# The seven products of a Strassen-Winograd unit summed in PSUM on ScalarE's copies, with two sums left to VectorE

## The chip, the cores and the metric

One core of one Trainium2 chip runs the whole program in one launch. The metric is device time in microseconds (us), from the core's own clock; three runs of the kernel before gave 543.16, 543.61 and 543.85 us, median 543.61. A profile is one execution, and its span runs from the first instruction to the last.

## The reference, cut to what matters

```python
# attention, batch 2, 12 heads, 448 tokens, head dimension 64, causal
attn = softmax(where(mask, -1e9, q @ k.T / 8)); x = (attn @ v)   # -> 896 x 768
# gated layer: 768 -> 1536 -> 768
xn = x / sqrt(mean(x * x) + 1e-6) * rms_g
x = (silu(xn @ w_gate) * (xn @ w_val)) @ w_out
# bilinear layer: 768 -> 1024, then two linear maps
h = ((x @ w1) * (x @ w2)) @ w3
return h @ w_out                                              # 896 x 768, float32
```

## The kernel before, in words

Tokens lie along the free axis: a tile is 128 features by 448 tokens of one batch, and everything after attention comes in such tiles. Every float32 operand is split into a high float16 part and a low bfloat16 part, and a product of two operands is three matmuls (high·high, high·low, low·high). `halve` makes the parts of a tile (`hi_part`, L448, on ScalarE or VectorE; `lo_part`, L452/L453, on VectorE or GpSimd).

The two layers' first maps and the very last one come as 2x2 blocks: two blocks of weights (gate and value, or w1 and w2) by two batches. `wino` (L832) computes such a 2x2 block product by the Strassen-Winograd scheme in 7 products in place of 8. There are 23 of these units: 12 of the gated layer (`unit`, weights `wgv`; called the gate stage), 8 of the bilinear layer (`wab`; the bilinear stage) and 3 at the end (`funit`; the last stage). A product of the first 20 units is 9 matmuls of 128x448 columns, of the last three 12. `w_out` of the gated layer between them (the `wo` stage) is computed plainly, in 12 groups of 36 matmuls. A unit's weights are loaded as 64-bit words, rebuilt to float32 (`fetch`, L464 to L473: a DMA, two VectorE operations and one that runs on ScalarE at L469 or on VectorE at L471), summed into the weights' Winograd combinations (`sums`, through `tt`: L487 on VectorE, L488 on GpSimd) and halved.

`wino` before: each of the seven products goes into its own PSUM bank (`mm_b`, eight banks in turn). ScalarE copies the first product to SBUF (`evict`, L847), and VectorE adds the others to running sums in SBUF (`join`, L850): seven joins in a unit, five of the products joined once and one of them twice. So a product waits for its bank to be free and for nothing else of its unit.

W' = w3 @ w_out does not depend on the input rows and is computed beside attention (`w_prime`; 16 groups of 24 matmuls of 128x384, all in the one bank of `g_b`, evicted by ScalarE at L521). The attention of a pair of heads (`pair`) is twelve calls; `norm(b)` closes a batch: it takes the row norms (squares at L673 on ScalarE), transposes the rows on TensorE, and forms the batch's inputs `xs` and their combinations (L705, L710, L736). `mix` does the same after the `wo` stage.

What sets the order: nothing is issued in the order of the source. `add` records each operation with an engine (some with a second one), an estimated duration, what it reads and writes, and a priority. `Plan.order` is a list scheduler: it runs a forward pass and a backward pass alternately (`PASSES` = 8 times), keeps the best, and issues every operation in the planned order. TP, WP0, WPS, GVS, OS, AS, FS and the dictionary PO hold the starting priorities; they were fitted together. Every engine then works through its own queue in that fixed order.

Of the kernel before, what the change touches and what calls it, by code (L numbers as in the profile page):

```python
# [40 lines left out]
TP = 27.6196  # L41
WP0 = -239.098
WPS = 45.6507
GVS = 3.3215
OS = 5.5733
AS = 2.8104
FS = -2.3605
PO = dict(dq=75.1441, dv=-34.3235, vh=-105.6002, vl=46.2211, sc=-50.0374, s3=-49.1818, hA=-126.5569,
    hl=33.2591, hB=-20.1561, pv=4.1734, sq=-72.0513, nm=15.7476, wm=1.3462, ww=-44.1947, wx=4.9061,
    g=68.9761, a=-39.7332, o=0.6949, f=-24.4064, gm=-31.525, e=-8.003, ae=-133.6189, y=-21.9007,  # L50
    t1=-54.0072, mx=44.5005, dw=-92.7682)
# [213 lines left out]
def actp_us(n):  # L265
    return n * 0.00083 + 0.055
# [14 lines left out]
def fused_kernel(ctx: ExitStack, tc, qk, v, g, wgv, wo, wab, w3t, wout, out):  # L281
# [208 lines left out]
    def mm(*a, **k):  # L490
        nc.tensor.matmul(*a, **k)  # L491
# [278 lines left out]
    def mm_group(ps, kp, terms, n, prio):  # L770
        for c in range(0, len(terms), n):
            def f(c=c):
                for q in range(c, min(c + n, len(terms))):
                    a, bb = terms[q][0]
                    k = 3 * q
                    for x0, x1 in ((a[0], bb[0]), (a[0], bb[1]), (a[1], bb[0])):
                        mm(ps[:, :S], x0, x1, start=(k == 0), stop=(k == 3 * len(terms) - 1))
                        k += 1
            ch = terms[c:c + n]
            add("pe", 3 * len(ch) * mm_us(S), f, r=[k for t in ch for k in t[1]], w=[kp], prio=prio)  # L780

# [49 lines left out]

    def wino(w, x, n, pr):  # L832

        (e1, k1), (c11, k11) = kp_r.next(), kp_r.next()
        (u3, k3), (c22, k22), (c21, k21) = (ew_r.next() for _ in range(3))

        def prod(ws, s, p):
            ps, kp = mm_b.next()
# [4 lines left out]
            mm_group(ps, kp, terms, 3, p)  # L843
            return ps[:, :S], kp

        def evict(dst, kd, ps, kp, p):
            add("act", actp_us(S), lambda: nc.scalar.activation(dst, ps, AF.Copy), r=[kp], w=[kd], prio=p)  # L847

        def join(dst, kd, ps, kp, y, ky, p):
            add("dve", dve_us(S), lambda: nc.vector.tensor_tensor(dst, ps, y, op=ALU.add), r=[kp, ky], w=[kd], prio=p)  # L850

        evict(e1, k1, *prod(0, 0, pr), pr)
        join(c11, k11, *prod(1, 1, pr), e1, k1, pr)
        pr += PO["gm"]
        join(e1, k1, *prod(4, 4, pr), e1, k1, pr)
        join(u3, k3, *prod(5, 5, pr), e1, k1, pr)
        five = prod(3, 3, pr)
        join(c22, k22, *five, u3, k3, pr)
        join(e1, k1, *five, e1, k1, pr)
# [126 lines left out]
```

## Time and profile before

| | before |
|---|---|
| median of three runs (lowest, highest) | 543.61 us (543.16, 543.85) |
| span of the profiled execution | 540.7 us |
| what the median has beside that span | 2.9 us |
| instructions | 9343 |
| TensorE (PE) busy | 527.1 us, 97%, 3516 matmuls |
| VectorE (DVE) busy | 487.1 us, 90%, 923 |
| ScalarE (ACT) busy | 363.6 us, 67%, 540 |
| GpSimd (POOL) busy | 179.3 us, 33%, 137 |
| mean granted TensorE clock | 1.000 |

The profiled execution's own time is told by its span alone; the 2.9 us are the launch and the end around it, by the runs' median.

How to read it: a busy share is a mean over stages. PE at 97% means little by itself, since matmuls are pipelined and their ends are modelled; whether PE really works at its pace is seen from the number of matmuls in a stretch, and whether it waits is seen from the list of waits and the chain. On the chain, a piece "PE x1926" means that PE went from one matmul to the next 1926 times without waiting for anyone.

### The profile page before, as it was taken

To read this page: it belongs to the slowest core of one execution; us is meant where nothing else is said; L and a number is where in the kernel's file an instruction comes from. 1 tells how busy PE (TensorE), PEld (TensorE's weight loads), DVE (VectorE), ACT (ScalarE), POOL (GpSimd) and SP (SyncE) were. 2 spreads that over 40 slices of the span, in tenths; PEclk is the share of its full clock that TensorE was granted. 3 is DMA by queue.
4 is the path that set the end of the run, shared out by engine and by line. 5 is a ranking of instruction groups with operands and counts; after the bars stand their busy time and mean duration, and the time that the engine had idled before them with its cause. 6 is when DMAs were issued, how large, how long until landed. Compare 5 with 4: busy or idle time off the path is not lost.

```text
span 540.7 us, 9343 instructions
## 1 busy us (share of the span) xinstructions
PE 527.1 (97%) x3516; PEld 293.4 (54%) x3516; DVE 487.1 (90%) x923; ACT 363.6 (67%) x540; POOL 179.3 (33%) x137
## 2 busy tenths in 40 slices
PE   8899999999988999999999999999999999999997
PEld 6556566565655555555555555555555555555553
DVE  6889999999958999999999998889769999999943
ACT  6899999999768766758565778797336543453310
POOL 4001214144226727573853310000100734556300
PEclk9999999999999999999999999999999999999999
DMA  8886768999931152433333347525105111000121
GB/s 277 303 300 210 258 246 184 239 234 202 204 99 58 59 176 73 161 116 117 118 118 116 118 176 241 226 91 203 58 1 174 60 60 58 1 0 1 52 86 68
DMA packets 46813, 74.92 MB, mean 139 GB/s; under 512 B 31408, under 2 KB 32944, under 8 KB 46768
## 3 DMA queue, kind: packets, MB, share of 16 engines
q1 hardware_dynamic: 46768, 74.33, 45.1%
q8 instruction: 27, 0.44, 0.3%
q14 instruction: 18, 0.15, 0.1%
HBM read 64.23 MB, written 2.75 MB: 124 GB/s over the span
## 4 chain that ended last, share of the span: by engine, by line
PE 81%; DVE 7%; ACT 5%; DMA 4%; issue 2%; SPq 0%; ACTq 0%; DVEq 0%
PE bank L491 80%; DMA st<-in_wout 2%; DVE arena L452 1%; ACT st L469 1%; PE bank L600 1%; ACT arena L448 1%; DMA arena<-arena 1%; DVE arena L560 1%; DVE cv L473 1%; DMA st<-in_wgv 1%; DVE cv L466 1%; DMA arena<-in_v 1%; ACT arena L736 1%; ACT arena L564 1%; ACT arena L673 0%
## 5 line engine op out<-in xcount | busy, mean ns | idle before, releaser
L491 PE MATMUL bank<-arena 128*128 128x448 f16 (+10 forms) x2976 | 441.8, 315 | 7.0 <-DVE arena L560 2.5
L491 PEld LDWEIGHTS <-arena 128*128 128x128 f16 x3048 | 249.7, 98 | 218.6 <-issue 15.1
L469 ACT ACTIVATE st<-st 128x768 uint16<-128x768 uint16 (+2 forms) x75 | 120.8, 1645 | 25.8 <-DVE cv L466 23.2
L850 DVE TENSOR_TENSOR arena<-bank,arena 128x448 f32<-128x448 f32 x161 | 91.3, 611 | 15.1 <-PE bank L491 14.7
L448 ACT ACTIVATE arena<-arena 128x448 f16<-128x448 f32 (+2 forms) x96 | 57.0, 612 | 35.9 <-DVE arena L487 27.2
L473 DVE SCALAR_TENSOR_TENSOR cv<-st,cv 128x768 int32<-128x768 int32 (+2 forms) x84 | 72.7, 868 | 5.1 <-ACT st L469 4.4
L453 POOL TENSOR_TENSOR arena<-cv,arena 128x384 bf16<-128x384 f32 (+2 forms) x29 | 46.1, 1590 | 86.8 <-ACT arena L448 77.8
L491 PE MATMUL bank<-xs,arena 128*128 128x448 f16 x360 | 72.5, 352 | 2.0 <-DVE arena L705 2.0
L448 ACT ACTIVATE arena<-cv 128x384 f16<-128x384 f32 (+2 forms) x82 | 54.0, 670 | 23.7 <-PE bank L491 11.9
L453 POOL TENSOR_TENSOR arena<-arena 128x448 bf16<-128x448 f32 (+2 forms) x32 | 46.6, 1468 | 49.4 <-ACT arena L448 40.7
L466 DVE TENSOR_SCALAR cv<-st 128x768 int32<-128x768 int32 (+2 forms) x84 | 45.3, 547 | 12.2 <-DMA st<-in_wout 4.4
L452 DVE TENSOR_TENSOR arena<-arena 128x448 bf16<-128x448 f32 (+2 forms) x68 | 50.5, 753 | 1.8 <-ACT arena L448 1.4
L448 ACT ACTIVATE arena<-st 128x1536 f16<-128x1536 f32 (+1 forms) x25 | 34.4, 1381 | 19.5 <-DVE st L487 9.9
L452 DVE TENSOR_TENSOR arena<-cv,arena 128x384 bf16<-128x384 f32 (+2 forms) x55 | 44.2, 815 | 0.2 <-ACT arena L448 0.2
L564 ACT ACTIVATE arena<-arena 128x128 f32<-128x128 f32 (+3 forms) x84 | 41.6, 520 | 2.8 <-DVE arena L560 2.2
L487 DVE TENSOR_TENSOR arena<-arena 128x448 f32<-128x448 f32 x53 | 35.2, 677 | 3.8 <-ACT arena L896 3.8
L488 POOL TENSOR_TENSOR st<-cv,st 128x384 f32<-128x384 f32 x8 | 10.8, 1353 | 78.3 <-DVE st L487 78.3
L560 DVE CUSTOM_DVE_ANT_0 arena<-bank,arena 128x128 f32<-128x128 f32 (+3 forms) x84 | 35.9, 443 | 0.4 <-ACT arena L564 0.3
L452 DVE TENSOR_TENSOR arena<-st,arena 128x1536 bf16<-128x1536 f32 (+1 forms) x21 | 35.3, 1679 | 0.1
L491 PEld LDWEIGHTS bank<-arena 64*128 64x128 f32 (+2 forms) x288 | 25.8, 178 | 16.5 <-DVE arena L560 5.0
L488 POOL TENSOR_TENSOR arena<-arena 128x448 f32<-128x448 f32 x18 | 24.9, 1388 | 14.6 <-ACT arena L871 5.8
L871 ACT ACTIVATE arena<-arena 128x448 f32<-128x448 f32 x24 | 13.7, 575 | 19.1 <-DVE arena L850 19.0
(67 smaller groups left out, 311.3 us busy)
## 6 DMA issues: line engine op xcount, KB each, us to landing
st<-in_wgv SPq DMA_DIRECT2D x24, 768.0 KB, 4.4
st<-in_wab SPq DMA_DIRECT2D x16, 768.0 KB, 4.4
st<-in_wo SPq DMA_DIRECT2D x12, 768.0 KB, 5.8
st<-in_w3t SPq DMA_DIRECT2D x16, 512.0 KB, 5.1
st<-in_wout SPq DMA_DIRECT2D x16, 384.0 KB, 3.8
arena<-in_qk SPq DMA_DIRECT2D x12, 448.0 KB, 5.4
arena<-in_v SPq DMA_DIRECT2D x12, 256.0 KB, 3.7
out_t<-arena SPq DMA_DIRECT2D x12, 224.0 KB, 1.9
```

The lines of the kernel that those rows point to most:

```text
L448: add("act", act_us(n), lambda: nc.scalar.activation(hi, src, AF.Copy), r=r, w=w, prio=prio, alt=(("dve", dve2_us(n), lambda: nc.vector.te ...
L452: add("dve", dve_us(n), lambda: nc.vector.tensor_tensor(lo, src, hi, op=ALU.subtract), r=r, w=w, prio=prio, port=True, alt=(("pool", pool_ ...
L453: port=True, alt=(("pool", pool_us(n), lambda: nc.gpsimd.tensor_tensor(lo, src, hi, op=ALU.subtract)),))
L466: add("dve", dve2_us(n), lambda: nc.vector.tensor_scalar(cv, hi, 3, 0x3FFFFFFF, op0=ALU.logical_shift_left, op1=ALU.bitwise_and), r=[ks], ...
L469: add("act", ACT_TOP * n - 0.08, lambda: nc.scalar.activation(b[:, :, 2], b[:, :, 1], AF.Copy, scale=1.0 / 8192, bias=-8191.0 / 16384), w= ...
L473: add("dve", dve_us(n), lambda: nc.vector.scalar_tensor_tensor(cv, hi, -0x3FFFFFF9, cv, op0=ALU.bitwise_and, op1=ALU.bitwise_or), r=[ks], ...
L487: add("dve", dve_us(n), lambda: nc.vector.tensor_tensor(out, a, b, op=op), port=True, alt=(("pool", pool_us(n) + 0.1, lambda: nc.gpsimd.te ...
L488: ("pool", pool_us(n) + 0.1, lambda: nc.gpsimd.tensor_tensor(out, a, b, op=op)),), **kw)
L491: nc.tensor.matmul(*a, **k)
L560: add("dve", dve_us(w), lambda: nc.vector.tensor_tensor_reduce(out=sc[:, :w], in0=ss[:, :w], in1=m, scale=-CSC, scalar=3.0e38, op0=ALU.add ...
L564: add("act", act_us(w) + 0.1, lambda: nc.scalar.activation(dst, sc[:, :w], AF.Exp, bias=mx[:, c:c + 1], scale=-1.0), r=[ksc, kmx + (c,)], ...
L850: add("dve", dve_us(S), lambda: nc.vector.tensor_tensor(dst, ps, y, op=ALU.add), r=[kp, ky], w=[kd], prio=p)
```

## The change

`wino` takes five banks A, E, B, C, D for a unit. Product 0 starts A. ScalarE copies A into bank B (a `fork`, PSUM to PSUM). Product 3 goes to E, and ScalarE copies it out to SBUF as m3. Product 4 is accumulated on A (`fresh=False`: its first matmul doesn't clear the bank), a second fork copies A into C, product 1 is accumulated on B, product 5 on A, a third fork copies A into D, product 6 is accumulated on C, product 2 on D. B and D are then two finished blocks that lie in PSUM; VectorE adds m3 to C and to A, which gives the other two. The products' arithmetic order changes, not their number.

A matmul that accumulates needs the bank's written marks to be set. Where no matmul of these stages has written the target bank yet, one matmul is put ahead of the fork (`primed`); this happens for four banks in the whole program.

What follows a unit changes with it. In the gate stage the Silu of batch 0 reads PSUM and writes SBUF, and the multiplication of batch 0 (`times`) reads PSUM, so that it runs on VectorE alone; batch 1 is as before. In the bilinear stage ScalarE first copies batch 0's block to SBUF; in the last stage it copies two blocks to SBUF ahead of their DMA. All starting priorities have new values, and two are added (`fk` for forks, `pm` for the marking matmuls).

```diff
-TP = 27.6196
-WP0 = -239.098
-WPS = 45.6507
-GVS = 3.3215
...
+TP = 25.3479
+WP0 = -234.519
+WPS = 43.9438
+GVS = 8.3892
...
-    def mm_group(ps, kp, terms, n, prio):
+    primed = set()
+
+    def mm_group(ps, kp, terms, n, prio, fresh=True):
...
-                        mm(ps[:, :S], x0, x1, start=(k == 0), stop=(k == 3 * len(terms) - 1))
+                        mm(ps[:, :S], x0, x1, start=(fresh and k == 0), stop=(k == 3 * len(terms) - 1),
+                           skip_group_check=True)
                         k += 1
...
+        primed.add(kp)
...
+    def copy_out(dst, kd, ps, kp, p, func=AF.Copy, r=()):
+        add("act", actp_us(S), lambda: nc.scalar.activation(dst, ps[:, :S], func), r=[kp, *r], w=[kd], prio=p)
+
     def wino(w, x, n, pr):
 
-        (e1, k1), (c11, k11) = kp_r.next(), kp_r.next()
-        (u3, k3), (c22, k22), (c21, k21) = (ew_r.next() for _ in range(3))
-
-        def prod(ws, s, p):
-            ps, kp = mm_b.next()
+        A, E, B, C, D = (mm_b.next() for _ in range(5))
+        m3, k3 = ew_r.next()
+
+        def prod(ws, s, dst, fresh, p):
...
-            mm_group(ps, kp, terms, 3, p)
-            return ps[:, :S], kp
...
-        evict(e1, k1, *prod(0, 0, pr), pr)
-        join(c11, k11, *prod(1, 1, pr), e1, k1, pr)
+            mm_group(*dst, terms, 3, p, fresh)
+
+        def fork(dst, src, p):
+            if dst[1] not in primed:
+
+                primed.add(dst[1])
+                (wi, kw), (x0, kx0) = w(0, 0), x(0, 0, 0)
+                add("pe", mm_us(S), lambda: mm(dst[0][:, :S], wi[0], x0, start=True, stop=True,
+                                                skip_group_check=True),
+                    r=[*kw, kx0], w=[dst[1]], prio=p + PO["pm"])
+            add("act", actp_us(S), lambda: nc.scalar.activation(dst[0][:, :S], src[0][:, :S], AF.Copy),
+                r=[src[1]], w=[dst[1]], prio=p + PO["fk"])
...
+        prod(0, 0, A, True, pr)
+        fork(B, A, pr)
+        prod(3, 3, E, True, pr)
+        copy_out(m3, k3, *E, pr)
         pr += PO["gm"]
-        join(e1, k1, *prod(4, 4, pr), e1, k1, pr)
-        join(u3, k3, *prod(5, 5, pr), e1, k1, pr)
-        five = prod(3, 3, pr)
-        join(c22, k22, *five, u3, k3, pr)
-        join(e1, k1, *five, e1, k1, pr)
-        join(c21, k21, *prod(2, 6, pr), u3, k3, pr)
-        join(e1, k1, *prod(6, 2, pr), e1, k1, pr)
-        return (c11, k11), (c21, k21), (e1, k1), (c22, k22)
+        prod(4, 4, A, False, pr)
+        fork(C, A, pr)
+        prod(1, 1, B, False, pr)
+        prod(5, 5, A, False, pr)
+        fork(D, A, pr)
+        prod(6, 2, C, False, pr)
+        prod(2, 6, D, False, pr)
+        return B, D, join(*C, pr, kp_r), join(*A, pr, ew_r)
+
+    def times(e, ke, u, ku, pr):
+        add("dve", dve_us(S), lambda: nc.vector.tensor_tensor(e, u[:, :S], e, op=ALU.mult), r=[ku], w=[ke], prio=pr)
...
+        e, ke = kp_r.next()
+        copy_out(e, ke, g0, kg0, pr, AF.Silu, ["exp"])
+        add("act", act_us(S), lambda g1=g1: nc.scalar.activation(g1, g1, AF.Silu), r=["exp"], w=[kg1], prio=pr)
+        times(e, ke, u0, ku0, pr)
+        tt(g1, u1, g1, ALU.mult, r=[ku1], w=[kg1], prio=pr)
```

## Rows read from the trace of the kernel before

**Rows 1.** The page's first part: engine, busy us (share of the span), instructions.
```profile
PE 527.1 (97%) x3516; PEld 293.4 (54%) x3516; DVE 487.1 (90%) x923; ACT 363.6 (67%) x540; POOL 179.3 (33%) x137
```
**Rows 2.** The chain that ended last, in order of time: start, us, what.
```profile
30.19 9.46 PE bank L491 x70
...
157.03 0.38 ACT wpr L521
157.42 0.04 issue
157.46 4.07 PE bank L491 x24
...
172.65 364.51 PE bank L491 x1926
537.18 0.62 DVE arena L850
```
**Rows 3.** Everything that PE waited for: us in total, times, longest.
```profile
PE bank L491 <- DVE arena L560: 2.5, 3, 1.7
PE bank L491 <- DVE arena L705: 2.0, 1, 2.0
PE bank L491 <- ACT wpr L521: 1.9, 3, 0.9
PE bank L491 <- DMA arena<-arena: 1.5, 2, 1.1
```
**Rows 4.** Stages: start:end, length, then each engine's busy us (and instructions).
```profile
0.00:30.19 30.19, 25.77 (x183) 17.45 (x184) 22.84 (x57) 23.92 (x38) 5.56 (x19) 1.00 0.88 297
30.19:81.42 51.23, 51.23 (x448) 31.48 (x448) 48.91 (x146) 49.79 (x88) 8.82 (x8) 1.00 0.74 246
81.42:172.65 91.23, 85.59 (x962) 56.14 (x961) 80.95 (x219) 78.65 (x163) 35.46 (x29) 1.00 0.81 180
172.65:312.00 139.35, 139.35 (x737) 72.11 (x737) 137.71 (x199) 93.35 (x114) 78.61 (x50) 1.00 0.34 114
312.00:394.00 82.00, 82.00 (x436) 42.39 (x434) 70.07 (x106) 59.47 (x67) 3.66 (x2) 1.00 0.46 164
394.00:490.00 96.00, 96.00 (x509) 49.68 (x508) 92.44 (x144) 46.81 (x59) 37.79 (x24) 1.00 0.15 50
490.00:537.20 47.20, 47.14 (x250) 24.17 (x247) 33.60 (x57) 11.66 (x16) 9.41 (x8) 1.00 0.15 55
```
**Rows 5.** Groups by shape, whole span: line, engine, shapes, count, busy us, mean ns.
```profile
L850 DVE TENSOR_TENSOR arena<-bank,arena 128x448 f32<-128x448 f32 x161 | 91.3, 611 | 15.1 <-PE bank L491 14.7
L847 ACT ACTIVATE arena<-bank 128x448 f32<-128x448 f32 x23 | 12.9, 559 | 19.0 <-PE bank L491 18.1 <-DVE arena L452 0.5 <-POOL arena L453 0.4
L521 ACT ACTIVATE wpr<-bank 128x384 f32<-128x384 f32 x16 | 7.9, 494 | 0.4 <-PE bank L491 0.4
L736 ACT ACTIVATE arena<-bank,gcol 128x448 f32<-128x448 f32 x9 | 5.7, 636 | 0.2 <-DVE xs L705 0.2
```
**Rows 6.** ScalarE's longest groups in the gate stage alone, 172.65 to 312.
```profile
L469 ACT ACTIVATE st<-st 128x768 uint16<-128x768 uint16 x18 | 34.4, 1940 | 11.3 <-DVE cv L466 10.9
L448 ACT ACTIVATE arena<-st 128x1536 f16<-128x1536 f32 x10 | 14.8, 1491 | 7.2 <-DVE st L487 7.1
```
**Rows 7.** Timeline at one copy of a first product: start, us, engine, what.
```profile
435.78 0.92 PE L491 MATMUL bank<-xs,arena 128*128 128x448 f16 x4
...
436.53 1.87 PE L491 MATMUL bank<-arena 128*128 128x448 f16 x9
436.79 0.54 ACT L847 ACTIVATE arena<-bank 128x448 f32<-128x448 f32 x1 [1.30 <-PE bank L491]
```
**Rows 8.** Timeline of ScalarE and of VectorE just ahead of 172.65.
```profile
167.13 1.94 ACT L469 ACTIVATE st<-st 128x768 uint16<-128x768 uint16 x1
168.79 1.11 ACT L448 ACTIVATE arena<-arena 128x448 f16<-128x448 f32 x2
169.78 0.65 ACT L710 ACTIVATE arena<-bank,gcol 128x448 f16<-128x448 f32 x1
...
170.46 1.27 DVE L705 SCALAR_TENSOR_TENSOR arena<-bank,gcol,arena 128x448 f32<-128x448 f32 x2 [1.23 <-ACT arena L710]
```
**Rows 9.** Timeline of ScalarE as the last heads end.
```profile
149.85 1.92 ACT L469 ACTIVATE st<-st 128x768 uint16<-128x768 uint16 x1
151.50 0.59 ACT L521 ACTIVATE wpr<-bank 128x384 f32<-128x384 f32 x1
...
156.94 0.47 ACT L521 ACTIVATE wpr<-bank 128x384 f32<-128x384 f32 x1
```

More of the change, by code (lines that the diff above doesn't have):

```diff
@@ L37 @@
 CSC = 1.0 / 8.0
-TP = 27.6196
-WP0 = -239.098
-WPS = 45.6507
-GVS = 3.3215
[L45 to L51, printed above, removed]
+TP = 25.3479
+WP0 = -234.519
+WPS = 43.9438
+GVS = 8.3892
+OS = 1.5337
+AS = 6.4345
+FS = -18.5115
+PO = dict(dq=296.1492, dv=10.4926, vh=-34.7118, vl=126.6907, sc=-72.5533, s3=-52.6832, hA=-202.3671,
+    hl=39.8475, hB=-61.5241, pv=16.197, sq=-136.1802, nm=-36.3792, wm=-26.2698, ww=-49.3707, wx=0.5906,
+    g=81.8494, a=-5.8385, o=8.5203, f=76.1736, gm=-209.9897, e=-104.2641, ae=56.8155, y=-53.6644,
+    t1=-102.0152, mx=-11.7701, dw=-150.6905, fk=-4.8427, pm=73.2581)
 PASSES = 8
@@ L842, in prod @@
                 terms.append(((wi, (x0, x1)), kw + [kx0, kx1]))
-            mm_group(ps, kp, terms, 3, p)
-            return ps[:, :S], kp
[L846 to L850, printed above, removed]
-        evict(e1, k1, *prod(0, 0, pr), pr)
@@ new lines, in join @@
+        def join(ps, kp, p, ring):
+            d, kd = ring.next()
+            add("dve", dve_us(S), lambda: nc.vector.tensor_tensor(d, ps[:, :S], m3, op=ALU.add), r=[kp, k3],
+                w=[kd], prio=p)
+            return d, kd
+        prod(0, 0, A, True, pr)
+        fork(B, A, pr)
+        prod(3, 3, E, True, pr)
+        copy_out(m3, k3, *E, pr)
+        pr += PO["gm"]
+        prod(4, 4, A, False, pr)
+        fork(C, A, pr)
+        prod(1, 1, B, False, pr)
+        prod(5, 5, A, False, pr)
@@ L867, in fused_kernel @@
         unit(wgv[f], f % 3, pr + PO["g"])
-        c11, c21, c12, c22 = wino(uw(f % 3), xs, 3, pr)
+        (g0, kg0), (u0, ku0), (g1, kg1), (u1, ku1) = wino(uw(f % 3), xs, 3, pr)
         pr += PO["e"]
-        for b, ((e, ke), (u, ku)) in enumerate(((c11, c21), (c12, c22))):
-            add("act", act_us(S), lambda e=e: nc.scalar.activation(e, e, AF.Silu), r=["exp"], w=[ke], prio=pr)
-            tt(e, u, e, ALU.mult, r=[ku], w=[ke], prio=pr)
-            part(e, ke, hset, b, f, pr)
+        e, ke = kp_r.next()
[3 more added lines that the diff above has]
+        tt(g1, u1, g1, ALU.mult, r=[ku1], w=[kg1], prio=pr)
+        part(e, ke, hset, 0, f, pr)
+        part(g1, kg1, hset, 1, f, pr)
     T2 = T1 + NF * step
@@ L909, in fused_kernel @@
         unit(wab[i + h * 4], r, pr + PO["a"])
-        c11, c21, c12, c22 = wino(uw(r), xs, 3, pr)
+        (a0, ka0), (b0, kb0), (a1, ka1), (b1, kb1) = wino(uw(r), xs, 3, pr)
         pr += PO["ae"]
-        for (e, ke), (u, ku) in ((c11, c21), (c12, c22)):
-            tt(e, u, e, ALU.mult, r=[ku], w=[ke], prio=pr)
+        e, ke = kp_r.next()
+        copy_out(e, ke, a0, ka0, pr)
+        times(e, ke, b0, kb0, pr)
+        tt(a1, b1, a1, ALU.mult, r=[kb1], w=[ka1], prio=pr)
+        c11, c12 = (e, ke), (a1, ka1)
         part(*c11, abset, h, i, pr)
@@ L925, in fused_kernel @@
             d, b = i + n % 2 * 3, n // 2
+            if n < 2:
+                ps, kp = e, ke
+                e, ke = kp_r.next()
+                copy_out(e, ke, ps, kp, pr)
             add("sp", dma_us(P * S * 4), lambda e=e, b=b, d=d: nc.sync.dma_start(
```

## The prediction

> **What bounds the kernel now.** The page's first part [rows 1] names two candidates, PE at 97% and DVE at 90%. The chain of waits decides between them, so it is read next. Its last long piece is PE alone: 1926 matmuls in 364.51 us, from 172.65 to 537.16, then one join and the output's DMA [rows 2]. That is 0.1893 us a matmul for 448 columns, and the list of waits has nothing that could lie in it: PE's waits [rows 3] are few, and the stages [rows 4] show PE busy without a gap in every window from 172.65 to 490. So DVE, though busy for 137.71 of 139.35 us in the gate stage, never makes PE wait there. Two thirds of the time are PE's own pace. What is left is ahead of it: PE runs without a break from 30.19 to 81.42, and loses 91.23 - 85.59 = 5.64 us between 81.42 and 172.65 [rows 4]. The first 30 us are loading and starting, and the change has no part in them.
>
> The Trainium skill gives the same pace a reason (TensorE: Matmul & The Clock Gate, "Wait — 56ns, not 53.3ns?"): columns divided by 2.4 GHz and about 2.5 ns, an estimate of 0.1892 us for 448. By that rule nothing done to the joins can shorten the 364.5 us, and the trace's 0.1893 at a granted clock of 1.00 agrees.
>
> **The change part by part.** All against the profiled span of 540.7 us; the runs' median is 2.9 us above it, and I add that at the end.
>
> *Joins taken from DVE.* A unit had 7, 161 in all, and keeps 2: 115 go. One costs 91.3/161 = 0.567 us of DVE's busy time [rows 5], so DVE loses 65 us, 34 of them in the gate stage. On the path that is 0: from 172.65 to 537 PE never waits for DVE. Twenty multiplications (`times`) can no longer go to GpSimd, at most 20 x 0.567 = 11 us back on DVE, again beside PE's work.
>
> *Copies given to ScalarE.* Before: 23. After: 69 forks, 23 of m3, 8 of the bilinear stage and 6 of the last stage, 106; 83 more at 12.9/23 = 0.561 us [rows 5] are 47 us of ScalarE. In the gate stage it was busy for 93.35 of 139.35 us; three more copies in each of 12 units make it 113.5, or 81%, if the planner moves nothing to DVE. A copy from PSUM to PSUM is not in the trace. Its nearest rows are the copy to SBUF, 0.559, below it the narrower one of L521, 0.494, and above it the scaled one of L736, 0.636 [rows 5]. I take 0.544, the duration in rows 7; either end moves only where a fork is exposed.
>
> *The new wait of PE.* This is the one thing that the change adds to the path. Products 4 and 5 go into A and may not start before the fork that reads A is done; products 1, 6 and 2 need their fork's output. The round trip: the group whose last matmul started at about 435.78 + 3 x 0.189 = 436.35 was copied from 436.79 on, 0.44 us later, by a ScalarE that was idle [rows 7]; the copy takes 0.54; from a ScalarE copy's end to PE's next matmul it is 0.05 (157.41 to 157.46 in [rows 2]). So 1.03 us from the last matmul of the source to the first that depends on it. In the order of the change another product of 9 matmuls lies between, which ends its issue 1.89 us after that same last matmul. So 0.86 us are spare, and with an idle ScalarE a fork costs nothing. It costs when the fork queues behind something long. ScalarE's longest operation, L469, takes 1.94 us (18 in the gate stage), and a halving of 1536 columns 1.49 (10) [rows 6]: a fork that comes just after one of these started is late by up to 1.94 - 0.86 = 1.08 or 0.63 us. L469 fills 34.4/139.35 = 25% of that stage. A fork that falls on it at random exceeds the spare time with 1.08/1.94 = 0.56, by 0.54 on the mean: 0.25 x 0.56 x 0.54 = 0.075 us. The halvings give 0.11 x 0.42 x 0.32 = 0.014. So 0.09 us x 36 forks = 3.2 us in the gate stage, if PE has nothing else to do. The other stages have few of these operations. But PE mostly has something else: the next unit's banks A, E and B are three that this unit doesn't hold, and the planner puts such products in between, since it knows L469's duration.
>
> Bounds. Below: 0. Above: the one place in the trace where PE waits for ScalarE to empty a bank that it needs again is W' with its single bank, where 16 groups gave 3 waits and 1.9 us [rows 3], 0.12 us each; 69 forks at this rate are 8.3 us. There ScalarE was busy for 97 and 86% (second and third line of [rows 4]), here for 81 at most, so I take 1.0 us, nearer to the lower end, and keep both.
>
> *Marking matmuls.* Four at 0.189 us: 0.8 us on PE. They could fall into a gap, so 0 to 0.8; I take 0.8.
>
> *What DVE's and ScalarE's relief can give ahead of 172.65.* The new priorities reorder everything, so this is the least certain part. In the 5.64 us that PE loses there, 1.96 are its wait for L705 just ahead of 172.65. L705 had waited 1.23 us for L710, and L710 stood in ScalarE's queue behind an L469 of 1.94 us, which rebuilds weights of a unit that is not due yet [rows 8]. In the same way an L469 stood at 149.85 ahead of an eviction of W' at 151.50, and the eviction at 156.94, with 0.9 us of PE's waiting, stood behind the squares that came late by it [rows 9, 3]. Before, this work had to be early: DVE was full from 172.65 on, and each unit's weights cost it more than it could spare later. With 34 us freed in the gate stage the second unit's weights can wait. What can be got: at most 5.64. The two waits for DMA transposes, 1.5 us [rows 3], are not touched by it. I count the wait for L705 whole (2.0), the longest for W' (0.9) and half of what is left of W' (0.5): 3.4 us. Below: nothing, or a loss by the reordering, which is a rival.
>
> *The end.* Before, the last product was followed by a join of 0.62 us and the DMA [rows 2]; after, by ScalarE's copy of 0.54, or a join. 0 within 0.1.
>
> Sum: 540.7 - 3.4 + 1.0 + 0.8 = 539.1, and with the 2.9 around it 542.0 us, 0.3% faster.
>
> **The rivals.**
>
> *A. PE's pace hides it all.* The gaps ahead of 172.65 stay, the forks cost nothing, the marking matmuls 0 to 0.8: 543.6 to 544.4. For it: in 364.5 us PE waits for nobody, so there is nothing to win where DVE's 65 us fall. Against it: [rows 8] show unit work ahead of the critical normalisation.
>
> *B. Forks behind long ScalarE operations.* Each engine keeps its planned order, so PE can't step round a late fork on the chip. At half of W's rate, 0.06 x 69 = 4.1 us, with the marking matmuls and no gain: 548.6; at the full rate 552.7. It decides from about 0.06 us a fork on. For it: ScalarE goes from 67 to 81% in the gate stage. Against it: 0.86 us of spare time at each fork, and no wait at all in 161 joins before.
>
> *C. The refitted order loses ahead of 172.65.* W' has 16 groups of 24 matmuls, 4.07 us each [rows 2], that fill PE there; if one more of them is left over and its slot stays empty, all after it ends later: 543.6 + 0.8 + 4.1 - about 1 = 547.5. For it: TP and W's step fall by different shares. Against it: the operations ahead of 172.65 are the same.
>
> *D. Forks bare.* If a product follows its fork without another between, PE stands for 1.03 - 0.19 = 0.84 us at each of 69 forks: 58 us, about 602. The Trainium skill speaks for such an end (Perfetto Trace Analysis, "Matmuls"): matmul groups should go round different PSUM banks, so that one's evacuation lies beside the next one's matmuls, and here three products of a unit follow each other in A. By that rule the time is D's. Against D: the order puts product 3, 1 or 6, in another bank, behind each fork.
>
> **How the numbers follow.** A measurement of this kernel tells about 0.2% from no change, here 1.1 us: below 542.5 is faster, above 544.7 slower. Forecast 0.45, of which 0.02 end within 0.2%; A 0.24; B 0.17; C 0.12; D 0.02. So faster 0.43, same 0.26, slower 0.31. The likeliest case by itself reaches from 538.8 (the whole 5.64 and 0.8 of marks) to 542.8. The range takes in A, C and B at half of W's rate: 538.8 to 549.0; above it lie the rest of B and D, below it hardly anything, as PE's own work ends there.
>
> **What would show it.** Right: 161 joins become 46, ScalarE has 106 such copies, DVE falls by 50 to 65 us, PE's long piece still goes at 0.189 us a matmul and starts 2 to 4 us earlier; PE's list of waits has ScalarE's forks with about 1 us. Wrong: a long piece that is broken many times by waits for forks (B, D), or one that starts at 172 or later (A, C). If the long piece starts much earlier than 169, my reading of what fills PE ahead of it is wrong.

## The result and the profile after

The changed kernel takes 547.77 us (median of 4 runs, 546.35 to 548.87); the kernel before, beside it, 543.52 us (4 runs, 543.16 to 543.85). The ratio is 1.007, 95% interval 1.005 to 1.0091: slower by 0.5 to 0.9%, more than the 0.2% that a measurement tells from no change. I had forecast 542.0. One disturbed run, e3's of 574.42 us, is left out of the medians.

The profiled execution has a span of 546.0 us, 5.3 more than before. That is 1.0 more than the medians differ. The changed kernel's profiled execution took 547.74 us, near its median, so 1.7 us lie around its span; in the other runs of both kernels it is 1.7 to 1.8 too. By this the profiled execution of before took some 542.5 us, 1.0 below its median. First part of the page, changed kernel; it answers to [rows 1]:

```profile
PE 529.0 (97%) x3526; PEld 294.5 (54%) x3526; DVE 443.0 (81%) x836; ACT 395.9 (73%) x618; POOL 142.3 (26%) x114
```

The relief is there: DVE has 44 us less, POOL 37 less, ACT 32 more. Span less PE's busy time is 17.0 us, before 13.6: PE stands still 3.4 us longer and is busy 1.9 us longer, with ten more matmuls: the four that mark banks, and six that only keep PE going in the first 30 us (L438, 106 in place of 100). Groups on the page (line, operation, shapes, count; busy us, mean ns; idle time before them), in place of L850 and L847 in [rows 5]:

```profile
L859 ACT ACTIVATE bank<-bank 128x448 f32<-128x448 f32 x69 | 37.9, 551 | 30.0 <-PE bank L491 27.9
L864 DVE TENSOR_TENSOR arena<-bank,arena 128x448 f32<-128x448 f32 x46 | 27.9, 618 | 28.8 <-ACT bank L859 24.2
L837 ACT ACTIVATE arena<-bank 128x448 f32<-128x448 f32 x49 | 26.9, 550 | 20.2 <-PE bank L491 19.0
```

L859 is the fork, L837 the copy out (12 of the 49 are the Silu of batch 0), L864 the join. PE's waits in the changed kernel, answering to [rows 3]:

```profile
PE bank L491 <- ACT wpr L521: 3.5, 6, 0.9
PE bank L491 <- ACT bank L859: 2.0, 3, 0.7
PE bank L491 <- DMA arena<-in_qk: 1.8, 1, 1.8
PE bank L491 <- DVE arena L705: 1.6, 2, 1.1
PE bank L491 <- DVE arena L665: 1.4, 1, 1.4
```

Three of the 69 forks make PE wait, 2.0 us together. The list is longer elsewhere too: W' 3.5 us where it was 1.9, L665 is new, and the wait for in_qk, which [rows 3] leaves out, was this in the kernel before:

```profile
PE bank L491 <- DMA arena<-in_qk: 0.6, 1, 0.6
```

The end of the chain, answering to [rows 2]:

```profile
264.11 1.84 ACT st L469
265.95 0.44 ACT bank L859
266.39 0.04 issue
266.43 276.05 PE bank L491 x1458
...
542.50 0.54 ACT arena L837
```

PE's pace is the same, 276.05/1458 = 0.1893 us. What is new is that PE's last undisturbed piece begins at 266.43, behind a fork, and not at 172.65. That fork on the timelines of PE and of ScalarE (start, us, what; in brackets the wait before it):

```profile
263.85 1.87 PE L491 MATMUL bank<-xs,arena 128*128 128x448 f16 x9
266.43 0.92 PE L491 MATMUL bank<-arena 128*128 128x448 f16 x4 [0.71 <-ACT bank L859]
```
```profile
263.58 0.53 ACT L859 ACTIVATE bank<-bank 128x448 f32<-128x448 f32 x1
264.04 1.91 ACT L469 ACTIVATE st<-st 128x768 uint16<-128x768 uint16 x1
265.70 0.68 ACT L859 ACTIVATE bank<-bank 128x448 f32<-128x448 f32 x1
```

The product of 9 matmuls that lies between gives its spare time, and the fork still comes 0.71 us too late, because the L469 ahead of it on ScalarE takes 1.91. The wait at 248.53 (0.62 us) is the same picture behind the L469 of 246.11. The third, at 189.84 (0.70), is behind a copy out and a halving. Two stages, answering to the second and third of [rows 4] (start:end, length, each engine's busy us):

```profile
30.19:81.42 51.23, 48.62 (x423) 30.08 (x423) 44.95 (x133) 47.06 (x81) 8.64 (x8) 1.00 0.72 232
81.42:172.65 91.23, 86.73 (x968) 56.63 (x965) 79.22 (x220) 76.95 (x161) 40.68 (x29) 1.00 0.81 179
```

In the stage where I looked for a gain PE stands still for 4.50 us, before 5.64: 1.1 were gained. In the one ahead of it, where it had run without a break, it now loses 2.6.

The list counts a wait from the modelled end of the last matmul. From start to start the pause at 266.43 is longer than PE's pace by 266.43 - 263.85 - 9 x 0.189 = 0.87, and the three forks' pauses together by 2.5, not 2.0.

The last matmul of the units starts at 542.11 (536.79 before). Of these 5.3 us the marking matmuls are 4 x 0.189 = 0.76 and the forks' pauses 2.5. Another 1.7 are there at 175 us: before had issued 31 matmuls of the units by then, the changed kernel 22, three marking ones among them, and 9 x 0.189 = 1.7. The rest, 0.3, lies in small pauses. What happens ahead of 175 us is what most of the experiments ask.

### The profile page after: what moved, and what is told of

Its sections match the earlier page's. It is cut to its first block, busy times and chain, and to the rows that moved or that the text cites. A ratio compares the mean times of both kernels' runs of the same rounds, so it can differ in the third digit from the quotient of the medians.

```text
span 546.0 us, 9311 instructions
## 1 busy us (share of the span) xinstructions
PE 529.0 (97%) x3526; PEld 294.5 (54%) x3526; DVE 443.0 (81%) x836; ACT 395.9 (73%) x618; POOL 142.3 (26%) x114
## 4 chain that ended last, share of the span: by engine, by line
PE 51%; ACT 3%; DVE 2%; issue 1%
PE bank L491 51%; ACT arena L448 1%; ACT st L469 1%; DVE arena L452 1%; ACT bank L859 1%; DVE st L487 0%; ACT arena L837 0%; DVE arena L864 0%; DVE arena L487 0%; DVE cv L466 0%; ACT arena L893 0%; DVE cv L473 0%
## 5 line engine op out<-in xcount | busy, mean ns | idle before, releaser
L491 PE MATMUL bank<-arena 128*128 128x448 f16 (+8 forms) x2976 | 442.9, 316 | 10.1 <-ACT wpr L521 3.5
L491 PEld LDWEIGHTS <-arena 128*128 128x128 bf16 (+1 forms) x3052 | 250.7, 98 | 222.3 <-issue 21.6
L469 ACT ACTIVATE st<-st 128x768 uint16<-128x768 uint16 (+2 forms) x71 | 114.0, 1627 | 7.1 <-DVE cv L466 5.5
L859 ACT ACTIVATE bank<-bank 128x448 f32<-128x448 f32 x69 | 37.9, 551 | 30.0 <-PE bank L491 27.9
L864 DVE TENSOR_TENSOR arena<-bank,arena 128x448 f32<-128x448 f32 x46 | 27.9, 618 | 28.8 <-ACT bank L859 24.2
L452 DVE TENSOR_TENSOR arena<-cv,arena 128x768 bf16<-128x768 f32 (+2 forms) x55 | 44.3, 806 | 4.7 <-ACT arena L448 4.6
L453 POOL TENSOR_TENSOR arena<-arena 128x448 bf16<-128x448 f32 (+2 forms) x20 | 35.0, 1758 | 44.5 <-ACT arena L448 44.5
L564 ACT ACTIVATE arena<-arena 128x384 f32<-128x384 f32 (+3 forms) x84 | 41.5, 524 | 2.6 <-DVE arena L560 2.2
L837 ACT ACTIVATE arena<-bank 128x448 f32<-128x448 f32 x49 | 26.9, 550 | 20.2 <-PE bank L491 19.0
L560 DVE CUSTOM_DVE_ANT_0 arena<-bank,arena 128x384 f32<-128x384 f32 (+3 forms) x84 | 35.7, 447 | 0.3 <-ACT arena L564 0.2
L488 POOL TENSOR_TENSOR st<-cv 128x384 f32<-128x384 f32 x9 | 11.8, 1312 | 89.6 <-DVE cv L473 87.1
L491 PEld LDWEIGHTS bank<-arena 64*128 64x128 f32 (+2 forms) x288 | 25.8, 180 | 16.2 <-DVE arena L560 4.5
```

The source lines that it names most:

```text
L452: add("dve", dve_us(n), lambda: nc.vector.tensor_tensor(lo, src, hi, op=ALU.subtract), r=r, w=w, prio=prio, port=True, alt=(("pool", pool_ ...
L453: port=True, alt=(("pool", pool_us(n), lambda: nc.gpsimd.tensor_tensor(lo, src, hi, op=ALU.subtract)),))
L469: add("act", ACT_TOP * n - 0.08, lambda: nc.scalar.activation(b[:, :, 2], b[:, :, 1], AF.Copy, scale=1.0 / 8192, bias=-8191.0 / 16384), w= ...
L560: add("dve", dve_us(w), lambda: nc.vector.tensor_tensor_reduce(out=sc[:, :w], in0=ss[:, :w], in1=m, scale=-CSC, scalar=3.0e38, op0=ALU.add ...
L564: add("act", act_us(w) + 0.1, lambda: nc.scalar.activation(dst, sc[:, :w], AF.Exp, bias=mx[:, c:c + 1], scale=-1.0), r=[ksc, kmx + (c,)], ...
L859: add("act", actp_us(S), lambda: nc.scalar.activation(dst[0][:, :S], src[0][:, :S], AF.Copy), r=[src[1]], w=[dst[1]], prio=p + PO["fk"])
```

## The experiments

All ratios are to the kernel before, run on the same chip. "Not busy" is the profiled span less PE's busy time, so what PE stood still.

| run | sums, order | median us (range, runs) | ratio, 95% interval | span | not busy |
|---|---|---|---|---|---|
| before | old | 543.52 (543.16 to 543.85, 4) | 1 | 540.7 | 13.6 |
| changed | new | 547.77 (546.35 to 548.87, 4) | 1.007, 1.005 to 1.0091 | 546.0 | 17.0 |
| e1 | new, before's priorities | 555.6 (555.28 to 557.28, 5) | 1.0236, 1.0208 to 1.0264 | 555.5 | 20.5 |
| e2 | old, changed priorities | 560.16 (558.64 to 563.47, 6) | 1.0321, 1.0286 to 1.0356 | 558.6 | 23.7 |
| e3 | new, forks of 8 columns | 545.09 (543.45 to 546.29, 11) | 1.0033, 1.0016 to 1.0051 | 543.3 | 15.2 |
| e4 | new, before's early order | 552.23 (550.64 to 553.93, 6) | 1.0161, 1.0133 to 1.0189 | 548.9 | 16.5 |
| e5 | new, changed again | 547.27 (545.58 to 548.64, 12) | 1.0057, 1.0035 to 1.008 | 544.7 | 16.3 |
| e6 | new, 6 forks earlier | 546.29 (544.81 to 547.22, 12) | 1.0039, 1.0018 to 1.0059 | 544.2 | 14.6 |
| e7 | old, own priorities 1 | 547.08 (543.9 to 550.05, 12) | 1.0053, 1.0024 to 1.0081 | 545.5 | 18.1 |
| e8 | new, own priorities 1 | 547.41 (544.82 to 551.02, 12) | 1.0059, 1.003 to 1.0087 | 546.2 | 16.2 |
| e9 | new, e6 and evictions of W' earlier | 547.42 (546.87 to 548.26, 6) | 1.0071, 1.0054 to 1.0087 | 545.5 | 13.8 |
| e10 | old, 7 operations moved | 546.18 (543.79 to 549.13, 12) | 1.0043, 1.0023 to 1.0062 | 545.7 | 15.2 |
| e11 | old, own priorities 2 | 553.53 (549.0 to 554.42, 6) | 1.0162, 1.0131 to 1.0193 | 547.2 | 19.6 |
| e12 | new, own priorities 2 | 546.35 (544.22 to 548.53, 8) | 1.0061, 1.004 to 1.0081 | 542.4 | 13.5 |
| e13 | new, room at forks 1 | 542.06 (540.71 to 545.14, 12) | 0.9967, 0.9947 to 0.9987 | 538.9 | 11.8 |
| e14 | new, room at forks 2 | 551.99 (551.59 to 552.93, 6) | 1.0148, 1.0121 to 1.0176 | 549.9 | 21.8 |
| e15 | new, first two loads exchanged | 547.63 (546.2 to 549.7, 6) | 1.008, 1.0056 to 1.0105 | 544.4 | 15.5 |
| e16 | old, first two loads exchanged | 543.76 (541.68 to 545.03, 12) | 0.9995, 0.9977 to 1.0013 | 542.3 | 13.5 |
| e17 | new, changed, third time | 547.33 (545.58 to 548.65, 6) | 1.007, 1.0046 to 1.0094 | 544.3 | 15.8 |
| e18 | new, e6 and loads exchanged | 546.28 (544.13 to 548.3, 11) | 1.0052, 1.0032 to 1.0072 | 544.5 | 15.0 |

**e1 and e2: sums and priorities apart.** e1 is the changed kernel with the constants of before, e2 the kernel before with those of the change.

```diff
-TP = 25.3479
+TP = 27.6196
...
-    t1=-102.0152, mx=-11.7701, dw=-150.6905, fk=-4.8427, pm=73.2581)
+    t1=-54.0072, mx=44.5005, dw=-92.7682, fk=0.0, pm=0.0)
```

> The change's summation in PSUM, with the starting priorities of the kernel before (the two new ones at 0). Theory R (the refit loses the time ahead of the long run of matmuls, the forks lose 2.0 us in it, the marking matmuls 0.8): the part ahead comes back to that of before, the long run starts near 172.6 us, and forks still cost 1 to 3: 545.3 to 547. Rival S (the new use of banks and of ScalarE makes every order worse): 547.8 or above, with the start of the long run as late as in the changed kernel or later.

> The summation of the kernel before, with the changed kernel's starting priorities. Theory R: the loss ahead of the long run is there without any fork, 543.5 + 2.5 = 546 or more (priorities fitted for another kernel may lose more), with no wait of PE inside the long run. Rival S: the priorities are harmless, 543 to 544.5.

Both are much slower than either kernel: e1 8 us above the changed kernel, e2 17 us above the kernel before. By the letter of the expectations e1 falls to rival S and e2 to theory R. But which half of the change costs time can't be read from such a pair, since a set of priorities is worth something only with the sums that it was fitted to. What e2 does show is that the old sums have no immunity. One of PE's waits in e2, then one stretch of it (the clock is the third number from the end):

```profile
PE bank L491 <- DVE arena L850: 4.2, 6, 2.0
```
```profile
170.00:200.00 30.00, 26.92 (x144) 15.85 (x143) 23.91 (x42) 22.41 (x31) 15.71 (x8) 0.89 0.13 49
```

With the same joins, six waits of PE are now for joins, where before none was.

**e3: short forks.** The changed kernel, each fork copying 8 columns in place of 448, so that the other columns of B, C and D lack the first products.

```diff
-            add("act", actp_us(S), lambda: nc.scalar.activation(dst[0][:, :S], src[0][:, :S], AF.Copy),
+            add("act", actp_us(S), lambda: nc.scalar.activation(dst[0][:, :8], src[0][:, :8], AF.Copy),
```

> The changed kernel in its own issue order, but each of the 69 forks copies 8 of 448 columns (what it leaves out: the sums of B, C and D lack the first product in the other columns). Theory R: the three waits of PE for forks, 2.0 us, fall below 0.6, since a fork takes some 0.2 us and not 0.53; the time falls by 1.4 to 2.0, to about 546. Rival (the waits come from what stands ahead of the fork on ScalarE, not from the fork's length): two of the three forks sit behind a 1.9 us operation, so the waits fall only by 0.35 each, to about 1.0, and the time by 1.0.

A fork takes 186 ns in place of 551, so 25 us of ScalarE's work are gone. The ratio is 1.0033 where the changed kernel's is 1.0057 to 1.007 (on other chips): 1.3 to 2.0 us. PE's waits in e3:

```profile
PE bank L491 <- ACT wpr L521: 2.9, 5, 1.3
PE bank L491 <- ACT bank L859: 1.8, 2, 1.0
```

Forks a third as long are still waited for (1.8 us, 2.0 to 2.2 in the unedited kernel): what stands ahead of a fork on ScalarE makes most of the wait, not its own length. So the 1.3 to 2.0 us are not explained by these waits, and where they come from isn't shown. And the ratio is still above 1: the forks' length alone doesn't make the loss.

**e5, e6 and e9: forks in front.** e5 is the changed kernel again. e6 has its order written out, with six forks of the gate stage moved ahead of their neighbours in ScalarE's queue; e9 moves eleven evictions of W' ahead as well. In all kernels with a written-out order the edit is this, and ORDER is the list:

```diff
-        return [f for _, f in sorted(issue, key=lambda x: x[0])]
+        return [filler if x == "f" else self.ops[int(x[:-1])][0][full[x[-1]]][1] for x in ORDER.split()]
```

> The changed kernel itself, unedited, so that e3 and the kernels beside it here have it on their own chip. 547 to 548 by its first measurement (ratio 1.007). If it comes near 545, most of what e3 gained was a difference between chips and not the shorter forks.

> The changed kernel's own order with six forks of the gate stage moved ahead of what stood before them on ScalarE (twice an L469, else halvings and a copy-out); the three that PE waited for are among them. Theory Q (the waits are the place in ScalarE's queue): PE's waits for forks go from 2.0 to below 0.5, and the time falls by 1.5 to 2.0 against the unedited kernel beside it. Rival (ScalarE as a whole is behind PE in the gate stage, whatever its order): the waits only move to other forks or to halvings, and the time stays within 0.6.

> As e6 (six forks moved ahead on ScalarE), and 11 of the 16 evictions of W' moved ahead of what stood before them on ScalarE too, wherever PE's source was done at least 0.4 us earlier. PE waits 3.5 to 4.1 us for these evictions in the changed kernel. Theory (PE's gaps ahead of the long run are its loss there): they fall below 1.5 and the time by a further 1.5 to 2.5 against e6, near before. Rival (ahead of the long run the heads' chain through VectorE and ScalarE sets the pace, and PE's gaps are only where its slack shows): the waits go, others take their place, and the time stays within 0.6 of e6.

PE's waits in e6, and the last piece of its chain:

```profile
PE bank L581 <- ACT wpr L611: 4.1, 6, 1.6
PE bank L581 <- ACT bank L949: 0.7, 2, 0.5
```
```profile
303.88 236.87 PE bank L581 x1251
```

(L949 is L859 there, L611 is L521.) The forks' waits go from 2.2 (e5) to 0.7 us, and the median falls from 547.27 to 546.29, 1.0 us. e15 and e18 below differ by the same edit, and by 1.35 us. The intervals of each pair overlap, so it is the repetition that speaks for it. In e9 the waits for W' fall from 4.1 to 2.2 us:

```profile
PE bank L581 <- ACT wpr L611: 2.2, 3, 1.2
```

No time comes of it (547.42, a ratio of 1.0071 where e6 has 1.0039, on another chip): a wait in that early part that is taken away need not be time that is won.

**e4 and e10: the waits ahead of the long run.** e4 gives the changed kernel an order written out, with before's order in the early part. e10 is the kernel before, with seven operations moved by hand: six evictions of W' ahead of their neighbours, and the L469 at 167.13 in [rows 8] behind the next L710. It is the prediction's own step, done alone.

> The changed kernel with a written-out issue order: attention, W', both normalisations and the weights of the first units in the order of the kernel before, everything behind in the order of the changed kernel, 2.5 us later in the plan. Theory R: it gets back what is lost ahead of the long run, 2.5 us, and keeps the forks and marks: 545.3, with the long run starting near 172.6. Rival S: the early loss comes back in another place (the weights or ScalarE are late in the gate stage): 547 to 548.

> The kernel before, its old sums and its own order, with two edits of ScalarE's queue: six evictions of W' moved ahead of what stood before them, and the L469 of 167.13 moved behind the L710 that VectorE and then PE waited for. It is the prediction's step on the 5.64 us ahead of the long run, done alone, without the change. If the step was right, PE's 2.0 us wait for L705 and most of its 1.9 for evictions go, and the kernel gets 2 to 3 us faster: 541 on a chip where before takes 543.5 to 544. Rival (those gaps are not what sets the start of the long run): within 0.6 of before.

e4 missed: where the two orders meet, PE waits 2.4 us for L736, the granted clock is 0.93 on the mean of 170 to 200 us, and the test doesn't tell what it was made for. In e10 neither wait goes away. PE's waits, the chain's end, two stretches and PE's timeline around the start of the long run (L797 is L705, L613 is L521):

```profile
PE bank L583 <- ACT wpr L613: 2.9, 2, 1.5
PE bank L583 <- DVE arena L797: 2.4, 1, 2.4
```
```profile
172.02 1.83 ACT st L561
173.85 0.83 ACT arena L540 x2
175.24 0.70 DVE arena L797
175.97 366.19 PE bank L583 x1926
```
```profile
176.00:180.00 4.00, 4.00 (x13) 1.73 (x13) 4.00 (x8) 3.70 (x8) 0.89 (x1) 0.57 0.00 0
180.00:184.00 4.00, 4.00 (x23) 2.08 (x22) 4.00 (x7) 3.99 (x6) 1.06 (x1) 1.00 0.43 145
```
```profile
171.53 2.00 PE L583 MATMUL bank<-arena 128*128 128x128 f32 x16
175.97 5.25 PE L583 MATMUL bank<-xs,arena 128*128 128x448 f16 x18 [2.44 <-DVE arena L797]
```

The waits for W' are 2.9 us, before 1.9. The wait for L705, 2.0 us before, is 2.4; the long run starts 3.3 us later than before; and another L469, the one of 172.02, stands in the chain to it. After the wait the granted clock is 0.57 in the first 4 us: 18 matmuls take 5.25 us where 18 x 0.1893 is 3.41. The time is 2.6 us above before. Part of it is the clock: four of the twelve runs have a mean granted clock of 0.999 or more and take 543.8 to 545.5 us, the other eight, at 0.993 to 0.997, 545.6 to 549.1. But the kernel before, beside it, takes 541.7 to 544.5 in its seven runs at 0.999 or more: e10 isn't faster at the full clock either.

**e15 to e18: the first loads.** One early difference is easily named. SyncE issues the first in_v ahead of the first in_qk in the changed kernel, and behind it before. PE waits 1.8 us for in_qk, and the clock of 10 to 15 us is 0.66 (1.00 before). e15 exchanges the two in the changed kernel, e16 in the kernel before, e18 in e6, and e17 is the changed kernel as it is.

```diff
-        return [f for _, f in sorted(issue, key=lambda x: x[0])]
+        out = [f for _, f in sorted(issue, key=lambda x: x[0])]
+        i, j = (out.index(ops[k][0]["sp"][1]) for k in (341, 342))
+        out[i], out[j] = out[j], out[i]
+        return out
```

> The changed kernel with one pair of neighbours in SyncE's queue exchanged: the first load of queries and keys (in_qk) is issued ahead of the first load of values (in_v), as in the kernel before. In the changed kernel's trace PE's first attention matmul stands at 9.99 us after a wait of 1.80 us for that load (8.81 and 0.61 before), and the granted clock in 10 to 15 us is 0.66 (1.00 before). Theory G (part of the loss that lies ahead of 172.65 is this start, the wait and the slower clock after it): the wait is back at about 0.6, the clock of that window at 1.00, and the time is 1.2 + 1.1 to 1.7 = 2.3 to 2.9 us below the unedited changed kernel on the same chip. Theory H (PE has to wait later anyway for W's weights and evictions, which soak this up): wait and clock are back too, but the time is within 0.7 us of the unedited one.

> The kernel before with the same two loads exchanged the other way: values ahead of queries and keys. Theory G: PE's first attention matmul waits about 1.8 us for the load, the clock of 10 to 15 us falls to about 0.66, and the time rises by 2.3 to 2.9 us over the kernel before. Theory H: within 0.7 us of it.

> The changed kernel, unedited, as the base for the runs beside it: 3 to 4.3 us above the kernel before by both theories (it was 3.2 and 4.2 above it in two earlier sets).

> The changed kernel's order with the six forks moved ahead on ScalarE (that was worth 1.0 us) and the two loads exchanged as well. Theory G: both gains add, 3.3 to 3.9 us below the unedited changed kernel, which is 0 to 1 us above the kernel before. Theory H: 0.5 to 1.7 us below the unedited one.

The time is as theory H has it in both directions: e15 against e17 +0.3 us, e16 against before -0.15 us, and e18 is at 1.0052 where e6 was at 1.0039. The stretches from 10 to 30 us, first of the changed kernel, then of e15:

```profile
10.00:15.00 5.00, 5.00 (x28) 3.32 (x29) 4.73 (x16) 4.72 (x10) 0.00 (x0) 0.66 0.94 320
15.00:30.00 15.00, 14.18 (x128) 9.57 (x127) 12.98 (x34) 14.03 (x22) 3.50 (x3) 1.00 0.94 317
```
```profile
10.00:15.00 5.00, 4.71 (x32) 2.89 (x30) 4.90 (x16) 4.73 (x9) 0.00 (x0) 1.00 0.92 308
15.00:30.00 15.00, 13.40 (x118) 9.13 (x117) 12.77 (x34) 13.65 (x22) 2.79 (x3) 1.00 0.91 317
```

The slower clock was not a matter of the order of the loads: e17, the changed kernel as it is, has 1.00 in that stretch (e5 has 0.66) and a wait of 1.1 us, and e16 keeps 1.00 though its PE waits 1.8 us. So this pair moves 1.1 and 1.2 us of waiting and leaves the clock alone. The last pieces of PE's chain, in e17, in e15 and in e16:

```profile
264.81 276.04 PE bank L491 x1458
```
```profile
264.92 276.03 PE bank L494 x1458
```
```profile
172.53 366.19 PE bank L494 x1926
```

e15 without the wait starts its last piece 0.1 us later than e17, and e16 with 1.2 us more of it starts the long run 0.1 us earlier than before (172.65). What was waited at the start was lost for nothing that follows: the 16 DMA engines are busy for 91 to 94% of 15 to 30 us, and PE, coming earlier, waits elsewhere. Two more things stand in these lines. e17 is the changed kernel unedited and starts the same 1458 matmuls 1.6 us earlier than the profiled execution above (266.43); by 175 us it had issued 31 matmuls of the units and e5 30, the marking ones among them, where that execution had 22 and before 31. So the 1.7 us that it had lost by then are not a property of the order. And e16's long run takes 1.7 us longer than that of before (366.19, 364.51): after the same wait of 1.96 us for L705 the granted clock is 0.59 from 172 to 176 us there.

**e7, e8, e11 and e12: other orders of the same sums.** New priorities, and new constants by which the planner chooses an operation's engine, for the old sums (e7, e11) and for the new ones (e8, e12), each found by a search that rates an order by the planner's estimated end; these orders were rated alike.

```diff
-TP = 25.3479
-WP0 = -234.519
...
+TP = 25.4905
+WP0 = -158.9887
...
```

> The kernel before with other starting priorities: a new random search, judged by the planner's own estimate alone, which rates this order a little better than that of before. Theory F (an order that is fitted on the estimate loses on the chip by chance, and before's order is a lucky one among its equals): 545 to 552, slower than before though nothing but the order differs. Rival S (the new use of banks and ScalarE is what loses): 542 to 544, as before.

> The changed kernel with starting priorities of another such search, rated a little better than its own. Theory F: anything from 543 to 552, as the order falls, and no worse as a group than the old sums' new orders. Rival S: 547 or more, always with waits for forks in the gate stage of 2 us or more.

> The kernel before with a third set of starting priorities, from a second search judged by the planner's estimate alone, rated a little better than before's. Theory F (before's order is a lucky one among its equals): 545 to 550, and PE waits in the long run though there is no fork. Rival S: 542 to 544.

> The changed kernel with a third set of starting priorities, from a second such search, rated like its own. Theory F: 544 to 550, no worse than e7 and e11 by more than the 0.8 of the marking matmuls and a fork wait or two. Rival S: 547 or more, above both of the old sums' new orders by 2 or more.

PE's waits inside the long run, in e7 and in e11, both with the old sums (L847 is the join L850, L844 the copy of the first product), and then those for forks in e8 (L856 is L859):

```profile
PE bank L488 <- DVE arena L847: 1.9, 3, 1.0
...
PE bank L488 <- ACT arena L844: 1.2, 2, 1.0
```
```profile
PE bank L488 <- DVE arena L449: 3.7, 3, 2.3
PE bank L488 <- DVE arena L847: 3.3, 2, 3.0
```
```profile
PE bank L488 <- ACT bank L856: 5.0, 6, 1.4
```

The old sums in three orders made for them: 543.5, 547.1 and 553.5 us. The new ones: 547.8, 547.4 and 546.4. Old sums that wait for nobody in 364 us are a property of one order, not of the sums. (The lines of e11 are from its fastest run, of 549.0 us.)

**e13 and e14: room at the forks.** The new sums; the planner counts 0.6 us more for a fork and 0.4 more for an eviction of W', so that it keeps other work away from them; priorities and the choice of engines searched anew.

```diff
-            add("act", actp_us(S), lambda: nc.scalar.activation(dst[0][:, :S], src[0][:, :S], AF.Copy),
+            add("act", actp_us(S) + 0.6, lambda: nc.scalar.activation(dst[0][:, :S], src[0][:, :S], AF.Copy),
```

> The changed kernel, with the planner made to count 0.6 us more for every fork and 0.4 us more for every eviction of W' than the copies take, and starting priorities from a search under these counts. Theory L (the new sums lose because the planner leaves no room where PE waits for a ScalarE copy, and an order with room loses nothing): PE's waits for forks below 0.7 us and for W' below 1, time 542.5 to 545. Rival S (the new sums lose by themselves, marks and forks): 546 or more. Rival F (each new order falls by chance, room or no room): 544 to 549, with other waits in the place of those.

> As e13 from another search with the same room at forks and evictions; the planner rates it a little lower than e13. Theory L: 543 to 546, waits for forks below 0.7 us. Rival S: 546 or more. Rival F: 544 to 549.

PE's waits in e13, and then those for forks in e14:

```profile
PE bank L488 <- ACT bank L856: 1.6, 3, 0.9
PE bank L488 <- DMA arena<-in_qk: 1.2, 1, 1.2
...
PE bank L488 <- DVE arena L702: 1.1, 1, 1.1
...
PE bank L488 <- ACT wpr L518: 0.9, 1, 0.9
```
```profile
PE bank L488 <- ACT bank L856: 5.4, 5, 1.9
```

e13 is faster than both kernels: 0.9967 of before, 0.9947 to 0.9987. Yet its waits for forks, 1.6 us, are not below the 0.7 that theory L asked for. e14, made in the same way, is 10 us slower than it and has 5.4 us of waits at the forks. So the room is not what makes e13 good; the new sums have orders on either side of before.

## Why the prediction was wrong

*PE's own pace bounds the time: right.* 0.1893 us a matmul in every long piece, before, after and in e10 (366.19/1926 = 0.190, with the slow stretch).

*Joins off DVE, copies onto ScalarE, worth 0 on the path: right.* 46 joins and 106 copies (69 forks and 37 copies out, beside 12 Silu on the same line) stand there as counted. DVE lost 44 us and not 50 to 65, with which POOL's 37 us less fit, as work that went over to DVE, and ScalarE gained 32 and not 47; nobody on the path feels it.

*A fork's duration, 0.544: right,* its median is 0.528 (517 to 715 ns over the 69), and none but the late ones matters.

*The new wait, 1.0 us: mechanism right, size too small.* 2.0 us in the list, and 2.5 from start to start, in 3 pauses, all in the gate stage, two of them behind an L469 as worked out; 2.7 in e5 and 2.8 in e17, where there are 3 and 4. Taking much of it away is worth 1.0 us (e6) and 1.35 (e18). e3 shows that the queue ahead of the fork, more than the copy, makes the wait. Rival B has this mechanism with a size of 4.1, which is too much for the order that was issued; e8 and e14 list 5.0 and 5.4, so another order of the same sums would have brought it.

*The marking matmuls, 0.8 us:* four were issued; their price is by PE's pace, and no run isolates it.

*The 2.9 us around the span: wrong.* Some 1.8 us lie around a span, and the other 1.1 were the profiled execution of before, which was faster than its median. With 1.8 the sum would have been 540.9.

*"What DVE's and ScalarE's relief can give ahead of 172.65", -3.4 us: this is the step that failed.* It was worth nothing. In the recorded execution the units were 1.7 us late at 175 us: 1.1 us less standing still in that stage, 2.6 more in the one ahead of it. In e5 and e17, the same kernel, they were 0.2 and 0 late, the marks aside. In the changed kernel PE waits 3.5 us for W' (1.9 before), 1.6 for L705 (2.0) and for things that were not on the list. The reasoning has two faults. First, I read from [rows 8] and [rows 9] which operation stood ahead of a late one, and took for granted that a refit would move just that. The refit rearranged all of it, with no regard for my list. Second, and worse, I took each listed wait for time that can be won. e10 moves the operations of my list by hand, in before's own order, and neither wait goes: another L469 takes the place, and the wait for L705 grows to 2.4. e15 and e16 remove and insert 1.1 and 1.2 us of waiting at the start, with 0.3 and -0.15 us of effect. e9 takes 1.9 us from the waits for W' and gains nothing. Ahead of 172.65 much of what PE waits at one place it would wait at another.

*The end, 0: right.* From the last copy's start to the end of the span it is 3.5 us (546.0 less 542.50), before also 3.5.

*The rivals.* A is out, PE's gaps changed. D is out: 66 of 69 forks cost nothing, since another product lies behind each. C gave 547.5, and that the median came out at 547.8 is luck: nothing of the length of its empty slot of W', 4.1 us, is in PE's waits, and what the recorded execution lost ahead of 175 us its repetitions did not lose. I had given C 0.12, because the operations there were the same. They were, and that says little: old sums spread from 543.5 to 553.5 us by their order and choice of engines alone, new ones from 542.1 to 552.0. Against that spread of 10 us the terms that I had worked out, 1.0, 0.8 and 3.4, are small.

The account can be drawn up at 175 us, behind which all kernels in this table have only matmuls of 448 columns. "Lost" is the time from there to the last matmul's start, less 0.1891 us (the mean of before) for each matmul; the new sums have four matmuls more.

| run | sums | matmuls of the units by 175 us | lost behind 175 us |
|---|---|---|---|
| before | old | 31 | 0 |
| changed | new | 22 | 2.9 |
| e5, e17 (the same) | new | 30, 31 | 3.1, 2.9 |
| e6 (forks moved, beside e5) | new | 27 | 2.1 |
| e15 | new | 30 | 2.8 |
| e18 (forks moved, beside e15) | new | 23 | 1.6 |
| e11 | old | 49 | 9.9 |
| e13 | new | 53 | 1.7 |

What is shown, then: the changed kernel pays 0.8 us by count for the marks and 2.9 to 3.1 behind 175 us, 2.5 to 2.8 of it in pauses at forks; that is the size of what its medians lose, 3.2 to 4.3 us in three sets of runs. Moving six forks takes 1.0 to 1.3 of it away, and the medians follow (e6, e18). The count at 175 us is of one execution each, and one order gave 22, 30 and 31. The relief that was to pay for this ahead of 172.65 didn't come. The loss doesn't lie in the new sums as such: e13 has them and is faster, being 22 matmuls or 4.2 us further at 175 us, the marks among them, and losing 1.7 behind it. But that needs no relief of DVE either: e11, with the old sums, is 18 matmuls or 3.4 us further, and loses more than that later. Whether the new sums are the better ones isn't shown: e13 is the best of five orders made for them, and the old sums had three. What stays open: what makes an order early at 175 us. Two candidates, single waits (e9, e10) and the first loads (e15, e16), didn't move the time; e4, meant to move the whole early order, was spoilt at its junction.

## What to carry to other kernels

Where a list scheduler orders everything, a change that refits it is two changes, and the second may be the larger: before crediting a gain to the first, re-time the old work in a few other orders that its planner rates alike, and take their spread as the uncertainty of any forecast. One profile is one execution: before a loss in it is explained, a second profile of the same kernel shows whether the loss is there again. A wait in the trace is time to be won only where nothing after it would wait instead; the test is to take away one such wait by hand in the old order, and it is cheap. A new wait on an engine's queue is priced by what may stand ahead of it there, not by its own length.

## What the runs showed of the hardware

- ScalarE's copy of 128x448 float32 from PSUM to PSUM takes 551 ns on the mean (528 in the median of the 69 in the changed kernel), where the copy to SBUF took 559 in [rows 5]; with 8 columns it takes 186 on the mean (e3).
- A gap of PE of some 2 us around 170 to 175 us can be followed by the lower level of TensorE's clock: 0.57 of full speed in the 4 us after 2.44 us of waiting in e10, 0.59 from 172 to 176 us after 1.96 us in e16. In the profiled execution of before the same wait of 1.96 us wasn't followed by it. In these kernels such a gap can cost 1.8 us (5.25 less 3.41) beside its own length, and whether it does differs between executions.
- The same kernel before ran from 541.4 to 546.4 us in 17 runs on one chip, and within 0.7 us in the first four; one order of the changed kernel had issued 22, 30 and 31 matmuls of the units by 175 us in three executions. Comparisons of 0.3% here need many runs, and the ratios to runs beside them.
